# Dense conv of block 1 between the first two tiles of block 0, half of block 0's cast on GpSimd with block 1's memsets behind it, fewer matmuls on zeros

## The chip, the cores and the metric

One core of a Trainium2 chip. The metric is the device time of one execution in microseconds; times quoted are medians over several executions, with lowest and highest. The profile's own span (first to last instruction) is about 1.8 us shorter than the time. Each kernel is compared with executions of the kernel before on the same chip.

## The reference, cut to what matters

```python
# a causal conv over the sequence, 7 taps, one softmaxed kernel for each of 8 heads of 24 channels
out = np.einsum('hk,bskhg->bshg', softmax(weight), x_unfolded)      # x: (8, 4160, 192)
# a maxout feed-forward on each of the 33280 tokens
h = np.maximum(np.maximum(x @ w1, x @ w2), x @ w3)                  # 192 -> 768
return h @ w_out                                                    # 768 -> 192
```

The kernel works in 65 blocks of 512 tokens. For each block it makes the conv as matmuls with a banded matrix, then six tiles of 128 hidden columns ("tiles" below), then the second matrix product. It uses max(a, b, c) = c + max(a-c, b-c, 0): wd holds w1-w3 and w2-w3, one relu on ACT and one max on VectorE (DVE in the profile) finish a tile.

## The kernel before: the parts that matter

The first four blocks are convolved "densely": x is cast from 32 to 16 bits in two interleaved halves xz[t][0] and xz[t][1], each with zeros where the other has data.

```python
def cast_dense(t, copies):                     # copies: an engine for each half
    ...
                    copy(out=xz[t][v]..., in_=xf...)           # 3 operations a half
def conv_dense(t, copies):                     # 60 small matmuls, then three copies to yd on ACT
    ...
def cross(t, cs=range(NC)):                    # VectorE: the other 64 partitions of yd
    ...
def l1(t, j, pools=...):                       # one tile: 6 matmuls, relu on ACT, max on VectorE
    ...
```

The order of the start (every engine works through its own instructions in program order):

```python
    for v in range(2):
        nc.gpsimd.memset(xz[1][v][:], 0.0)     # early, while x is still on its way
    ...
    cast_dense(0, (nc.vector.tensor_copy, nc.scalar.copy))
    ...
    copy_w3(nc.vector.tensor_copy, 0)
    make_wd(0, 1)
    conv_dense(0, (nc.scalar.copy, nc.scalar.copy, nc.scalar.copy))
    keep_warm(4)                               # 4 matmuls on zeros
    cross(0, (0,))
    make_wd(1, 2, nc.gpsimd)
    cross(0, (1, 2))
    l1(0, 0)
    cast_dense(1, (nc.gpsimd.tensor_copy, nc.scalar.copy))
    cast_w3(0)                                 # GpSimd, for the transposes of w3
    copy_w3(nc.vector.tensor_copy, 1)
    l1(0, 1)
    conv_dense(1, (nc.scalar.copy, nc.scalar.copy, nc.scalar.copy))
    keep_warm(3)
    cross(1)
    make_wd(2, 4)                              # VectorE: columns that the third tile needs
    l1(1, 0)
    ...
    l1(0, 2)                                   # "the third tile of block 0" below
```

The softmax here doesn't subtract the row's maximum and nothing guards it: scores larger than these inputs give would overflow.

Of the kernel before, what the change touches and what calls it, by code (L numbers as in the profile page):

```python
# [27 lines left out]
def kernel(  # L28
# [12 lines left out]
    nc = tc.nc  # L41
# [116 lines left out]
    xz = {t: [const.tile([P, NQ, D], FP16, name=f"xz_{t}_{v}") for v in range(2)] for t in range(2)}  # L158
    xz[2], xz[3] = xz[0], xz[1]

    def cast_dense(t, copies):
        xf, _, parts = xin[t]
        for v, copy in enumerate(copies):
            if copy is None:
                continue
            for s in range(CYC // 32):
                cut = GRP * (32 * s // GRP + 1)
                a, b = (32 * s, cut) if v == 0 else (cut, 32 * s + 32)
                for (rl, q0, q1) in parts:
                    copy(  # L170
                        out=xz[t][v][0:rl, q0:q1, :].rearrange("p q (k c) -> p q k c", c=CYC)[:, :, :, a:b],
                        in_=xf[0:rl, q0:q1, :].rearrange("p q (k c) -> p q k c", c=CYC)[:, :, :, a:b])
# [26 lines left out]
    make_identity(nc, ident[:])  # L199
    ident16 = const.tile([P, P], FP16)  # L200
    nc.gpsimd.tensor_copy(out=ident16[:], in_=ident[:])
    for v in range(2):
        nc.gpsimd.memset(xz[1][v][:], 0.0)
    for x16 in x16s + [x16z]:
        w = x16.shape[1] - EDGE
        nc.gpsimd.memset(x16[:, 0:EDGE], 0.0)
# [4 lines left out]
    def keep_warm(n, pool=psw, tag="w"):  # L211

        ps = pool.tile([P, NBLK], FP32, tag=tag, name="idle")
        for _ in range(n):
            nc.tensor.matmul(ps[:], lhsT=idle[:, 0:P], rhs=idle[:], start=True, stop=True)  # L215
# [15 lines left out]
    wrec = const.tile([NHEAD, 1], FP32)  # L231
    nc.vector.reciprocal(out=wrec[:], in_=wsum[:])
    nc.scalar.activation(out=line[:, 31:31 + KW], in_=wexp[:], func=AF.Relu, scale=wrec[:])
    cast_dense(0, (nc.vector.tensor_copy, nc.scalar.copy))
    bps = psq.tile([32, WIN, NHEAD], FP32, tag="q", name="band_cols")
    for c in range(WIN):
        nc.tensor.matmul(bps[:, c, :], lhsT=line[:, WIN - 1 - c:WIN + 31 - c],  # L237
# [14 lines left out]
    def make_wd(j0, j1, eng=nc.vector):  # L252
        f = slice(P * j0, P * j1)
        eng.tensor_sub(out=wd[:, :, f], in0=ws[:, :, f], in1=w3s[:, :, f])  # L254

    def copy_w3(copy, part):
        f = slice(PW * part, PW * (part + 1))
        copy(out=w3s[HALF:P, :, f], in_=w3s[0:HALF, :, f])  # L258

    def cast_w3(part):  # L260
        f = slice(PW * part, PW * (part + 1))
        nc.gpsimd.tensor_copy(out=w3h[:, :, f], in_=w3s[0:HALF, :, f])
# [45 lines left out]
    def conv_dense(t, copies):  # L308


        yd = dense[t] = ydp.tile([P, NC, NBLK], FP16, tag="yd", name=f"yd_{t}")
        for n, slots_ in enumerate((range(4), range(4, 6))):
            ps = psw.tile([P, NBLK], FP32, tag="w", name=f"D{n}_{t}")
            for (q, b, row_lo, rlen, lo, hi, cc) in chunks_of[t]:
                for v in range(2):
                    for g, s in enumerate(slots_):
                        h = (32 * s + 31 * v) // GRP
                        nc.tensor.matmul(  # L318
                            ps[32 * g:32 * g + 32, lo:hi],
                            lhsT=xz[t][v][0:rlen, q, 32 * s:32 * s + 32],  # L320
                            rhs=band[0:rlen, h, cc:cc + hi - lo],
                            start=(v == 0), stop=(v == 1), tile_position=(0, 32 * g))
            if n == 0:
                copies[0](out=yd[0:HALF, 0, :], in_=ps[0:HALF, :])
                copies[1](out=yd[HALF:P, 1, :], in_=ps[HALF:P, :])
            else:
                copies[2](out=yd[0:HALF, 2, :], in_=ps[0:HALF, :])

    def cross(t, cs=range(NC)):

        yd = dense[t]
        for c in cs:
            a, b = (slice(HALF, P), slice(0, HALF))[::-1 if c == 1 else 1]
            nc.vector.tensor_copy(out=yd[a, c, :], in_=yd[b, c, :])  # L334
# [30 lines left out]
    def l1(t, j, pools=((psp, "p"), (psq, "q"))):  # L365


        N, y = blkN[t], dense[t]
        ps = [pool.tile([P, NBLK], FP32, tag=tag, name=f"l{tag}{i}_{t}_{j}")
              for i, (pool, tag) in enumerate(pools)]  # L370
        for c in range(NC):
            for i in range(2):
                row = slice(HALF * i, HALF * (i + 1))
                nc.tensor.matmul(ps[i][:, 0:N], lhsT=wd[row, c, P * j:P * (j + 1)],  # L374
                                 rhs=y[row, c, 0:N],
                                 start=(c == 0), stop=(c == NC - 1))
        r = rp.tile([P, NBLK], FP16, tag="r", name=f"r_{t}_{j}")
        nc.scalar.activation(out=r[:, 0:N], in_=ps[0][:, 0:N], func=AF.Relu)  # L378
        nc.vector.tensor_max(out=hs[t][:, j, 0:N], in0=r[:, 0:N], in1=ps[1][:, 0:N])  # L379
# [81 lines left out]
    copy_w3(nc.vector.tensor_copy, 0)  # L461
    make_wd(0, 1)
    conv_dense(0, (nc.scalar.copy, nc.scalar.copy, nc.scalar.copy))
    keep_warm(4)
    cross(0, (0,))
    make_wd(1, 2, nc.gpsimd)
    cross(0, (1, 2))
    l1(0, 0)
    cast_dense(1, (nc.gpsimd.tensor_copy, nc.scalar.copy))
    cast_w3(0)  # L470
    copy_w3(nc.vector.tensor_copy, 1)
    l1(0, 1)
    conv_dense(1, (nc.scalar.copy, nc.scalar.copy, nc.scalar.copy))
    keep_warm(3)
    cross(1)
    make_wd(2, 4)
    l1(1, 0)
    cast_w3(1)
# [107 lines left out]
```

## Time and profile before

| | before |
|---|---|
| time, median (lowest to highest) | 474.73 us (474.59 to 475.15), 3 runs |
| span of the profiled execution | 472.5 us |
| TensorE's share of the chain that ended last | 98% |
| block 0's first copy to yd on ACT starts | 8.31 us |
| block 1's conv starts | 11.51 us, broken off until 12.17 |
| third tile of block 0 starts | 16.31 us |
| block 2's conv starts | 23.09 us |

The last rows are starts in the timeline of the engine concerned. How much later or earlier block 2's conv starts is the measure used below: behind it TensorE runs from matmul to matmul to the end. The chain, the engines' rows from 9 us on and the arrivals are shown in the prediction. One more piece of the timeline before, VectorE's, from the arrival of block 0's x on (columns: start, duration of the group, engine, line, operation, operands, count, wait before it):

```profile
4.50 0.55 DVE L170 CAST xz<-xf 112x240 f16<-112x240 f32 x3 [1.34 <-DMA xf<-in_x_dram]
5.34 0.69 DVE L258 COPY w3s<-w3s 64x768 f32<-64x768 f32 x1 [0.29 <-DMA w3s<-in_moe_w_dram]
7.42 0.56 DVE L254 TENSOR_TENSOR wd<-ws,w3s 128x384 f16<-128x384 f32 x1 [1.40 <-DMA ws<-in_moe_w_dram]
```

### The profile page before, as it was taken

What the parts mean: (1) busy time and instruction counts of PE and PEld (TensorE: products, weight loads), DVE (VectorE), ACT (ScalarE), POOL (GpSimd) and SP (SyncE); (2) the same over time, 40 slices, a digit from 0 to 9 for tenths busy, and PEclk for the clock granted to TensorE, in tenths of its full rate; (3) what the DMA queues carried; (4) which work ended last, traced back from release to release, by engine and by line L of the source; (5) the groups of instructions that cost most, each with busy time, mean ns of one, the idle gap of its engine ahead of it and who ended that gap; (6) DMA issues with size and microseconds to landing.
All of it is one profiled execution on the core that took longest, in us unless ns stands there. A gap on an engine that the chain in (4) does not pass through costs nothing.

```text
span 472.5 us, 21840 instructions
## 1 busy us (share of the span) xinstructions
PE 467.0 (99%) x9036; PEld 392.1 (83%) x9036; DVE 364.2 (77%) x607; ACT 326.1 (69%) x612; POOL 215.0 (45%) x349
## 2 busy tenths in 40 slices
PE   8999999999999999999999999999999999999996
PEld 4577888888888888888888888888888888888996
DVE  4878878778777787787877877778778787787775
ACT  5777767677676766766667667676676666766664
POOL 5746445345435435354534543543553454454210
PEclk9999999999999999999999999999999999999999
DMA  9956877666577566667666666756675765764423
GB/s 197 242 136 189 211 191 195 171 176 181 166 191 193 162 172 172 163 191 189 166 184 166 194 166 186 192 154 178 173 191 162 199 181 154 195 176 101 108 84 103
DMA packets 68257, 81.49 MB, mean 172 GB/s; under 512 B 9310, under 2 KB 57246, under 8 KB 68158
## 3 DMA queue, kind: packets, MB, share of 16 engines
q1 hardware_dynamic: 55070, 49.21, 42.1%
q0 software_dynamic: 12928, 30.78, 21.3%
q8 instruction: 71, 1.16, 1.1%
q14 instruction: 28, 0.23, 0.2%
q10 hardware_dynamic: 160, 0.10, 0.1%
HBM read 30.31 MB, written 25.56 MB: 118 GB/s over the span
## 4 chain that ended last, share of the span: by engine, by line
PE 98%; DVE 1%; issue 0%; ACT 0%
PE lp L374 32%; PE po L418 30%; PE lq L374 26%; PE G L299 7%; PE idle L215 1%; PE D L318 1%; PE lw L374 1%; DVE yd L334 0%; PE band_cols L237 0%; DVE h L379 0%; DVE w3s L258 0%; PE pm L282 0%; PE pm L278 0%; PE pt L269 0%; DVE o L428 0%
## 5 line engine op out<-in xcount | busy, mean ns | idle before, releaser
L379 DVE TENSOR_TENSOR h<-r,lq 128x512 f16<-128x512 f16 x386 | 264.5, 685 | 97.6 <-ACT r L378 96.6
L378 ACT ACTIVATE r<-lp 128x512 f16<-128x512 f32 x386 | 230.5, 597 | 134.3 <-PE lp L374 89.7
L374 PE MATMUL lp<-yd,wd 64*128 64x512 f16 x1158 | 311.8, 376 | 0.5 <-DVE yd L334 0.5
L374 PE MATMUL lq<-yd,wd 64*128 64x512 f16 x1158 | 311.4, 375 | 0.0
L418 PE MATMUL po<-wo,h 64*128 64x192 f16 x3120 | 230.2, 243 | 0.0
L418 PEld LDWEIGHTS <-h 64*128 64x128 f16 x3120 | 186.2, 94 | 25.8
L374 PEld LDWEIGHTS <-wd 64*128 64x128 f16 x2340 | 164.3, 93 | 21.9 <-issue 1.8
L447 POOL DMA_DIRECT2D out_dram<-o x64 | 51.2, 799 | 235.7 <-DVE o L428 223.7
L357 POOL DMA_DIRECT2D yd<-ys x183 | 92.0, 509 | 1.4 <-ACT ys L344 0.8
L418 PE MATMUL po<-m,yd 64*128 64x192 f16 x780 | 86.9, 243 | 0.0
L428 DVE TENSOR_TENSOR o<-a,po 128x384 f32<-128x384 f32 (+1 forms) x132 | 71.4, 542 | 1.0 <-ACT a L427 1.0
L427 ACT COPY a<-po 128x384 f32<-128x384 f32 (+1 forms) x132 | 61.7, 468 | 2.1 <-PE po L418 2.1
L418 PEld LDWEIGHTS <-yd 64*128 64x128 f16 x780 | 54.8, 94 | 8.1
L151 POOL CAST x<-xf 112x960 f16<-112x960 f32 x60 | 59.6, 995 | 1.5 <-DMA xf<-in_x_dram 1.4
L344 DVE CAST ys<-G 128x512 f16<-128x512 f32 x61 | 39.2, 683 | 0.0
L299 PEld LDWEIGHTS <-x 112*32 112x32 f16 x2400 | 28.6, 96 | 12.7 <-issue 12.3
L344 ACT CAST ys<-G 128x512 f16<-128x512 f32 x61 | 32.9, 588 | 1.3
L299 PE MATMUL G<-band,x 112*32 112x103 f16 (+1 forms) x2400 | 33.3, 209 | 0.0
L215 PE MATMUL idle<-idle 128*128 128x512 f16 x18 | 6.9, 532 | 1.2 <-DVE idle L210 1.2
L318 PEld LDWEIGHTS <-xz 112*32 112x32 f16 x240 | 4.7, 107 | 2.2 <-issue 1.3
L318 PE MATMUL D<-band,xz 112*32 112x103 f16 (+1 forms) x240 | 5.7, 229 | 0.1
L254 POOL TENSOR_TENSOR wd<-ws,w3s 128x384 f16<-128x384 f32 (+1 forms) x2 | 3.2, 1606 | 5.0 <-DMA ws<-in_moe_w_dram 5.0
(52 smaller groups left out, 55.3 us busy)
## 6 DMA issues: line engine op xcount, KB each, us to landing
xf<-in_x_dram SPq DMA_DIRECT2D x57, 420.0 KB, 4.6
out_dram<-o POOLq DMA_DIRECT2D x62, 384.0 KB, 4.2
yd<-yd SPq DMA_DIRECT2D x61, 192.0 KB, 3.1
yd<-ys POOLq DMA_DIRECT2D x61, 48.0 KB, 3.5
yd<-ys SPq DMA_DIRECT2D x61, 48.0 KB, 3.9
xf<-in_x_dram SPq DMA_DIRECT2D x8, 252.0 KB, 4.3
yd<-ys POOLq DMA_DIRECT2D x61, 32.0 KB, 3.3
yd<-ys SPq DMA_DIRECT2D x61, 32.0 KB, 3.6
```

Of the source, the lines that this page charges most:

```text
L151: nc.gpsimd.tensor_copy(out=v[0:rl, q0:q1, :], in_=xf[0:rl, q0:q1, :])
L299: nc.tensor.matmul(G[i][32 * g:32 * g + 32, lo:hi], lhsT=x16[0:rlen, cb:cb + 32], rhs=band[0:rlen, h, cc:cc + hi - lo], start=True, stop=T ...
L318: nc.tensor.matmul(ps[32 * g:32 * g + 32, lo:hi], lhsT=xz[t][v][0:rlen, q, 32 * s:32 * s + 32], rhs=band[0:rlen, h, cc:cc + hi - lo], star ...
L344: copy(out=slots[t][:, i, :], in_=convs[t][i][:])
L357: (nc.sync, nc.gpsimd)[n % 2].dma_start(out=yd[r0:r0 + rows, c, :], in_=slots[t][s0:s0 + rows, half, :])
L374: nc.tensor.matmul(ps[i][:, 0:N], lhsT=wd[row, c, P * j:P * (j + 1)], rhs=y[row, c, 0:N], start=(c == 0), stop=(c == NC - 1))
L378: nc.scalar.activation(out=r[:, 0:N], in_=ps[0][:, 0:N], func=AF.Relu)
L379: nc.vector.tensor_max(out=hs[t][:, j, 0:N], in0=r[:, 0:N], in1=ps[1][:, 0:N])
L418: nc.tensor.matmul(ps[b0, i][:, s % 2, :], lhsT=a, rhs=b, start=first, stop=last)
L427: nc.scalar.copy(out=a[:, ss, :], in_=ps[s0, 0][:, ss, :])
L428: nc.vector.tensor_add(out=outs[t][:, s0:s + 1, :], in0=a[:, ss, :], in1=ps[s0, 1][:, ss, :])
L447: qs[0].dma_start(out=bass.AP(tensor=out.tensor, offset=r * D, ap=[[D, n], [step * D, s1 - s0], [1, D]]), in_=ob[p0:p0 + n, s0:s1, :])
```

## The change

Its intent: ACT is a bottleneck of the start (cast, copies and relus in one queue), so block 0's half cast goes to GpSimd, with the two memsets of block 1's buffers moved from the very start to behind it; block 1's cast and conv move ahead of the second tile of block 0, so that block 1 is ready sooner; and two places get fewer matmuls on zeros.

```diff
-    for v in range(2):
-        nc.gpsimd.memset(xz[1][v][:], 0.0)
...
-    cast_dense(0, (nc.vector.tensor_copy, nc.scalar.copy))
+    cast_dense(0, (nc.vector.tensor_copy, nc.gpsimd.tensor_copy))
+    for v in range(2):
+        nc.gpsimd.memset(xz[1][v][:], 0.0)
...
     conv_dense(0, (nc.scalar.copy, nc.scalar.copy, nc.scalar.copy))
-    keep_warm(4)
+    keep_warm(2)
     cross(0, (0,))
     make_wd(1, 2, nc.gpsimd)
     cross(0, (1, 2))
+    cast_dense(1, (nc.gpsimd.tensor_copy, nc.scalar.copy))
+    copy_w3(nc.vector.tensor_copy, 1)
     l1(0, 0)
-    cast_dense(1, (nc.gpsimd.tensor_copy, nc.scalar.copy))
     cast_w3(0)
-    copy_w3(nc.vector.tensor_copy, 1)
+    conv_dense(1, (nc.scalar.copy, nc.scalar.copy, nc.scalar.copy))
+    cross(1)
     l1(0, 1)
-    conv_dense(1, (nc.scalar.copy, nc.scalar.copy, nc.scalar.copy))
-    keep_warm(3)
-    cross(1)
+    keep_warm(2)
     make_wd(2, 4)
     l1(1, 0)
```

## The prediction

> **What bounds the kernel now.** I read the page first, then the chain of waits in order of time over the first 60 us, then the timelines of ACT, DVE and POOL over the first 24 us. From the page:
>
> ```profile
> PE 467.0 (99%) x9036; PEld 392.1 (83%) x9036; DVE 364.2 (77%) x607; ACT 326.1 (69%) x612; POOL 215.0 (45%) x349
> ...
> PE 98%; DVE 1%; issue 0%; ACT 0%
> ```
>
> TensorE sets the end: 98% of the chain that ended last is matmuls. What isn't TensorE is a per cent or two of 472.5 us, and the diff touches only the start-up, so the question is where in the start-up TensorE stands still. The chain in order of time:
>
> ```profile
> 9.11 0.97 PE idle L215 x4
> ...
> 11.49 0.15 DVE h L379
> 11.65 0.56 issue
> 12.21 0.69 DVE w3s L258
> 12.93 0.69 DVE h L379
> 13.65 0.41 DVE yd L334
> 14.09 0.86 DVE yd L334
> 14.99 0.37 PE lp L374
> ```
>
> Between 11.49 and 14.99 us the chain leaves TensorE; before and after that it stays on it. (9.11 is the first of the two groups of matmuls on zeros that the change shortens; its name is "idle" but TensorE is occupied.) After 14.99 the chain runs from matmul to matmul to the end, with no wait that shows. So a gain is to be had only before about 16 us, and from there on every microsecond gained or lost is carried to the end, unless something else then arrives too late. Why the hole is there, ACT and DVE show:
>
> ```profile
> 10.86 0.60 ACT L378 ACTIVATE r<-lp 128x512 f16<-128x512 f32 x1 [0.76 <-PE lp L374]
> 11.36 0.77 ACT L170 CAST xz<-xf 112x80 f16<-112x80 f32 x3
> ...
> 12.82 0.58 ACT L324 CAST yd<-D 64x512 f16<-64x512 f32 x1 [0.20 <-PE D L318]
> ```
>
> ```profile
> 12.21 0.69 DVE L258 COPY w3s<-w3s 64x768 f32<-64x768 f32 x1
> 12.93 0.69 DVE L379 TENSOR_TENSOR h<-r,lq 128x512 f16<-128x512 f16 x1
> 13.65 1.61 DVE L334 COPY yd<-yd 64x512 f16<-64x512 f16 x3
> 15.29 0.96 DVE L254 TENSOR_TENSOR wd<-ws,w3s 128x768 f16<-128x768 f32 x1
> ```
>
> ACT's half of block 1's cast stands behind the first tile's relu (11.36 to 12.13), so block 1's dense conv begins at 11.51, stops, and goes on only at 12.17. Its three copies to yd end at 14.61, and DVE's three crossings at 15.26. DVE then makes columns 2 to 4 of wd until 16.25; the third tile of block 0 begins at 16.31. TensorE alone would be far ahead of that.
>
> The transfers set a second clock, seen at GpSimd:
>
> ```profile
> 9.72 0.90 POOL L170 CAST xz<-xf 112x240 f16<-112x240 f32 x3 [0.89 <-DMA xf<-in_x_dram]
> 10.57 1.59 POOL L262 CAST w3h<-w3s 64x768 f16<-64x768 f32 x2
> 13.09 0.82 POOL L258 COPY w3s<-w3s 64x768 f32<-64x768 f32 x1 [0.93 <-DMA w3s<-in_moe_w_dram]
> 13.98 0.82 POOL L262 CAST w3h<-w3s 64x768 f16<-64x768 f32 x1
> 16.07 1.84 POOL L254 TENSOR_TENSOR wd<-ws,w3s 128x768 f16<-128x768 f32 x1 [1.28 <-DMA ws<-in_moe_w_dram]
> 18.30 1.14 POOL L491 CAST wo<-wos 128x1152 f16<-128x1152 f32 x1 [0.39 <-DMA wos<-in_moe_w_out_dram]
> 20.01 3.40 POOL L170 CAST xz<-xf 112x240 f16<-112x240 f32 x12 [0.57 <-DMA xf<-in_x_dram]
> ```
>
> These starts are arrivals and won't move. wd's last columns are ready at 17.91 and first used at 19.26 (1.35 us to spare); wo at 19.44, used at 20.71 (1.27); the first six of the twelve casts end near 21.7 and block 2's conv begins at 23.09 (1.4). So TensorE can be at most about 1.27 us earlier whatever the change does.
>
> **What the Trainium skill says.** "SBUF — State Buffer", section "SBUF: two separate sides": VectorE's second pair of SBUF ports is GpSimd's only one, and whoever starts first, a VectorE operation that needs both pairs or a GpSimd one, holds it for the whole instruction. The trace agrees: the crossing copy takes 0.29 us at 8.93 and 9.53, when GpSimd rests, and 0.41 and 0.85 us at 13.65 and 14.09, under GpSimd's copy and cast of w3. "GPSIMD Engine Reference", section "Engine selection": one-input work runs roughly at line rate there. The trace agrees: its three casts of block 1 take 0.90 us, ACT's three of the same shapes 0.78. "TensorE: Matmul & The Clock Gate", "Part 1: The HAM clock gate": matmuls run at half rate until some 3.4 us of activity. The trace: the 512-column matmuls on zeros start 0.43 us apart at 1.2 us, 0.22 apart from 9.04. The change leaves TensorE's order before 9.04 as it was, so I expect the same moment of release, and gaps after it far shorter than 3.4 us.
>
> **The change part by part.**
>
> *Block 0's half cast from ACT to GpSimd, xz[1]'s memset behind it.* ACT loses 0.78 us at 4.45; its band copies then begin at once when the band matmuls end (5.03) instead of at 5.14: 0.1 us. But block 0's conv begins at 7.21, behind five matmuls on zeros that end there, while the band is ready at 6.77. Worth nothing. GpSimd's three casts (0.90) start at 4.45, share the ports with VectorE's three (0.55) and its copy of w3 (0.69), and are over before 6; the two memsets (1.73) end near 7.8. GpSimd's part of wd took 1.37 from 7.46; I read about 0.45 of that as waiting for VectorE's wd (768 columns took 1.84, so 384 should take 0.92), so it ends near 8.8 to 9.2 as before. Its use is after 11.9. Worth nothing either.
>
> *Two matmuls on zeros fewer before the first tile.* They are two of 0.22. But that tile's last matmul waits for the third crossing (10.13 + 0.38 = 10.51). It still starts at 10.56 and ends at 10.77. Worth nothing at the end of the tile.
>
> *Block 1's conv before the second tile.* ACT's casts come right after its third copy of block 0: 10.10 + 0.78 = 10.88 instead of 12.13. GpSimd's casts are done at 10.62. So the conv starts near 10.86, takes 1.03 (block 2's conv, warm: 1.02 in the chain) and ends near 11.9, against 13.1. First copy on ACT at 10.86 + 0.70 = 11.56 (block 2: 23.09 to 23.79), three to 13.35 (0.58 with a pitch of 0.60). That is 1.26 us earlier than 14.61. The second tile follows on TensorE, 11.95 to 12.65 (six matmuls, 0.65 a tile from 17.93, 18.61, 19.26), then two on zeros (0.43).
>
> *DVE, which then sets the pace.* New order: copy of w3's second part, first tile's max, three crossings, second tile's max, wd columns 2 to 4. The copy could begin at 10.53, but its data land near 10.56 (my estimate: between the arrivals at 9.72 and 13.09 lie four equal parts of w3, w1, w2, w3, so a quarter of 3.37 after 9.72) and GpSimd's cast of w3h holds the ports from 10.57 to about 11.25. So: copy to 11.95, max to 12.66, first crossing to 12.97, second to 13.28, third after ACT's 13.35 and behind GpSimd's delayed copy of w3, to 14.15. The second tile's relu on ACT is 13.37 to 13.96; its max 14.17 to 14.86; wd 14.88 to 15.85. The third tile of block 0 starts at 15.9 instead of 16.31. Sum: about -0.4 us. TensorE will have finished block 1's first two tiles and a transpose near 15.2 and wait 0.7 us there: most of the 1.26 us gained on ACT is lost because the second tile's max (0.69) has moved in front of nothing it helped: it now stands between the crossings and wd.
>
> From 15.9 the order of all engines is as before and every deadline above keeps over 0.8 us, so -0.4 us goes through to the end: 474.73 - 0.4 = 474.3.
>
> **The rivals.** (a) No collision on the ports: the copy of w3 runs 10.53 to 11.22, crossings end at 13.70, max runs from 13.98, wd ends at 15.65, the third tile starts at 15.7: -0.6, 474.1. For it: VectorE and GpSimd arrive within 0.05 us of each other, and the first wins. (b) Worse collisions: the copy waits for both casts of w3h (12.16) and two crossings for GpSimd's copy and cast at 13.09 to 14.80. Then the crossings end near 15.2, max 15.9, wd 16.9: +0.6, 475.3. Against it: at 13.65 VectorE got in between two GpSimd instructions (0.41), so one that waits isn't passed over twice. (c) The whole 1.26 us comes through, limited by wo to 1.27: 473.5. That needs wd's columns not to be what the third tile waits for; against it stands wd's end at 16.25 right before the 16.31 start. (d) The gain is hidden by transfers: block 2's conv waits for xz. Against: 1.4 us to spare.
>
> **Range and chances.** From rivals (a) and (b), -0.6 to +0.6 around -0.4, leaning to the gain, with (c) less likely; the three runs before spread 0.56 us. I take 473.5 to 475.0. Two per cent is 9.5 us, eight times what the start-up could give: within 2% at 0.98, 0.01 on either side.
>
> **What would show it right or wrong.** Right: block 0's conv still at 7.2 us; ACT's three casts of block 1 near 10.1; block 1's conv unbroken from about 10.9; ACT's copies of it end near 13.4; the chain goes through DVE (max, wd) just before the third tile of block 0 near 15.9; from there TensorE to the end, all shifted alike. Wrong: block 0's conv late behind GpSimd (its casts held up by VectorE), a crossing longer than 0.8 us, a TensorE wait for wo or for xz between 18 and 24 us, or 512-column matmuls 0.43 us apart after 9.1 us.

## The result, and the profile after

The changed kernel: 474.31 us median (473.60 to 474.67, 4 runs); the kernel before 474.74 (474.59 to 475.15, 4 runs, three of them those of the table above). The ratio of the two is 0.9988 with a 95% interval of 0.9970 to 1.0005. (Ratios are the mean time of one kernel's runs over that of the other's, so not quite the ratio of the medians quoted.) Executions over 1.5% slower than the fastest of the same kernel are left out of the means. The interval includes 1: the 0.43 us between the medians is not secured by these runs alone.

The profiled execution of the changed kernel took 474.56 us, longer than the profiled one of before (474.32). So this trace cannot be expected to show a gain, and it doesn't. Its chain of waits in order of time (start, duration, what):

```profile
1.19 3.48 DMA xf<-in_x_dram
4.80 2.78 DVE xz L170 x2
7.63 1.15 PE D L318 x28
8.80 0.58 ACT yd L324
...
15.04 0.46 DVE h L379
15.64 0.96 DVE wd L254
16.65 0.39 PE lp L374
```

The second half is as predicted: VectorE's max of the second tile, then wd, then the third tile of block 0. The first half is new. Before, the chain ran through matmuls on zeros at this place; now it starts with the arrival of block 0's x (4.80 us), goes through VectorE's cast of it, and block 0's conv can only then go on. VectorE's and GpSimd's rows:

```profile
4.80 2.88 DVE L170 CAST xz<-xf 112x240 f16<-112x240 f32 x3 [1.65 <-DMA xf<-in_x_dram]
7.71 0.69 DVE L258 COPY w3s<-w3s 64x768 f32<-64x768 f32 x1
8.43 0.56 DVE L254 TENSOR_TENSOR wd<-ws,w3s 128x384 f16<-128x384 f32 x1
...
10.83 1.30 DVE L258 COPY w3s<-w3s 64x768 f32<-64x768 f32 x1
12.17 0.69 DVE L379 TENSOR_TENSOR h<-r,lq 128x512 f16<-128x512 f16 x1
12.89 2.12 DVE L334 COPY yd<-yd 64x512 f16<-64x512 f16 x3
15.04 0.69 DVE L379 TENSOR_TENSOR h<-r,lq 128x512 f16<-128x512 f16 x1
15.64 0.95 DVE L254 TENSOR_TENSOR wd<-ws,w3s 128x768 f16<-128x768 f32 x1
```

```profile
4.83 0.98 POOL L170 CAST xz<-xf 112x80 f16<-112x80 f32 x3 [2.80 <-DMA xf<-in_x_dram]
5.75 1.73 POOL L234 MEMSET xz<- 128x960 f16 x2
8.48 1.36 POOL L254 TENSOR_TENSOR wd<-ws,w3s 128x384 f16<-128x384 f32 x1 [1.00 <-DVE w3s L258]
...
10.71 1.84 POOL L262 CAST w3h<-w3s 64x768 f16<-64x768 f32 x2
13.15 0.82 POOL L258 COPY w3s<-w3s 64x768 f32<-64x768 f32 x1 [0.60 <-DMA w3s<-in_moe_w_dram]
14.04 0.82 POOL L262 CAST w3h<-w3s 64x768 f16<-64x768 f32 x1
```

VectorE's three casts take 2.88 us instead of 0.55. Taken one by one, the second of them alone lasts 2.57 (the row gives shortest, median and longest of the three in ns, then first and last start and the shapes):

```profile
L170 DVE CAST xz<-xf x3: 183/285/2572, 4.8 to 7.5; 112x240 f16<-112x240 f32 x1, 112x160 f16<-112x160 f32 x1, 112x80 f16<-112x80 f32 x1
```

It ends at 7.57, just after GpSimd's last memset (7.48). GpSimd's casts and memsets have held it up. Later VectorE's copy of w3 takes 1.30 us (0.69 alone), and three crossings 2.12 (0.87 alone, three times 0.29), each time under GpSimd's casts and copies of w3.

What ACT makes of it:

```profile
8.80 0.58 ACT L324 CAST yd<-D 64x512 f16<-64x512 f32 x1 [2.08 <-PE D L318]
...
10.49 0.78 ACT L170 CAST xz<-xf 112x80 f16<-112x80 f32 x3
11.17 0.59 ACT L378 ACTIVATE r<-lp 128x512 f16<-128x512 f32 x1
11.98 0.58 ACT L324 CAST yd<-D 64x512 f16<-64x512 f32 x1 [0.22 <-PE D L318]
```

Block 0's first copy starts at 8.80 instead of 8.31, block 1's at 11.98 instead of 12.82. So the new order has brought block 1's copies 0.84 us forward even in this execution; of the 1.26 us predicted, the late start of block 0 took about 0.5. Collisions on VectorE then eat more than the 0.84 (the second and third crossing take 0.92 and 0.85 us), and the third tile starts at 16.65 against 16.31. From there on both traces run alike: block 2's conv at 23.44 against 23.09, and the last matmuls of the two end 0.41 us apart.

### The profile page after: what moved, and what is told of

Same layout as the page of the kernel before. It is cut to its first block, busy times and chain, and to the rows that moved or that the text cites. A ratio compares the mean times of both kernels' runs of the same rounds, so it can differ in the third digit from the quotient of the medians.

```text
span 472.8 us, 21832 instructions
## 1 busy us (share of the span) xinstructions
PE 466.7 (99%) x9033; PEld 391.3 (83%) x9033; DVE 367.8 (78%) x607; ACT 325.5 (69%) x609; POOL 217.1 (46%) x352
## 4 chain that ended last, share of the span: by engine, by line
PE 96%; DVE 2%; DMA 1%; issue 1%; ACT 0%; SPq 0%; DVEq 0%
PE lp L374 32%; PE po L418 30%; PE lq L374 26%; PE G L299 7%; DMA xf<-in_x_dram 1%; PE D L318 1%; DVE xz L170 1%; PE lw L374 0%; DVE yd L334 0%; DVE h L379 0%; DVE wd L254 0%; PE pm L282 0%; PE pm L278 0%; ACT yd L327 0%; ACT yd L324 0%
## 5 line engine op out<-in xcount | busy, mean ns | idle before, releaser
L170 POOL CAST xz<-xf 112x80 f16<-112x80 f32 (+2 forms) x18 | 5.2, 334 | 3.3 <-DMA xf<-in_x_dram 2.8
```

## The experiments

Theory P (ports): with GpSimd's cast and memsets beside it, VectorE's cast of block 0 waits until GpSimd rests; block 0's conv then starts a fixed time after x lands. The new order gains what was predicted, the cast's move loses part of it. The rival, theory C (chance): x came late in that one execution (4.80 us instead of 4.45) and the moved cast costs nothing.

All traces in one table, starts in us. "x" is VectorE's first cast of block 0, that is, x's arrival. The text refers to it throughout.

| kernel | x | block 0's first copy | block 1's conv | third tile | block 2's conv |
|---|---|---|---|---|---|
| before | 4.50 | 8.31 | 11.51 | 16.31 | 23.09 |
| before_again | 4.64 | 8.31 | 11.55 | 16.57 | 23.36 |
| changed | 4.80 | 8.80 | 11.27 | 16.65 | 23.44 |
| after_again | 4.62 | 8.64 | 11.10 | 16.51 | 23.30 |
| after_third | 4.67 | 8.69 | 11.36 | 16.56 | 23.35 |
| warm_back | 4.32 | 8.34 | 10.90 | 15.88 | 22.66 |
| order_only | 4.38 | 8.32 | 10.85 | 15.97 | 22.77 |
| order_only_2 | 4.45 | 8.32 | 11.06 | 15.99 | 22.78 |
| memset_early | 4.44 | 7.41 | 10.17 | 15.80 | 22.59 |
| cast_only | 4.25 | 7.87 | 11.20 | 16.59 | 23.38 |
| cast_only_2 | 4.42 | 8.44 | 11.55 | 16.32 | 23.10 |
| w3_pool | 4.33 | 8.32 | 10.83 | 15.87 | 22.66 |
| w3_pool_split | 4.51 | 8.32 | 10.78 | 15.68 | 22.58 |
| memset_twice | 5.14 | 9.13 | 12.47 | 19.25 | 26.04 |

In memset_early and cast_only the five matmuls on zeros ahead of block 0's conv end about 0.5 us earlier than elsewhere (conv from 6.7 instead of 7.2 us), so their second column isn't to be compared with the others'; after_third has that early end too, but there the conv is held up anyway. "The Trainium skill", page "TensorE: Matmul & The Clock Gate", section "Part 1: The HAM clock gate", says that TensorE's full rate comes with a window that runs free of the kernel, so that its moment varies from run to run, by 500 ns either way. These traces agree that it varies, but by more: by their clock records full rate begins at 4.06 to 4.34 us in those three (after_third falls back to half rate from 7.54 to 10.96) and at 8.17 to 12.82 in the other eleven. The five matmuls, 0.22 us apart in the three and 0.43 in the others, say the same.

### The changed kernel again (after_again, after_third)

No edit.

> The changed kernel once more, five rounds, to size the difference. Theory P (ports): with GpSimd casting half of block 0 and then clearing xz[1], VectorE's own cast of block 0 waits until GpSimd rests, and block 0's conv starts when that ends, so its start follows the arrival of block 0's x: 7.2 us when x lands at 4.45, 7.6 when it lands at 4.8. Then its times spread wider than those of before (about 1 us against 0.5), with a median 0.3 to 0.6 us under before. Theory C (chance): the late conv of the first profile was a late arrival and nothing else; then the median is about 1 us under before and a second profile shows VectorE's three casts done in about 0.6 us.

Measured: 474.25 us median of 6, one (481.82) slow; 474.20 for the five fast ones (473.88 to 475.10), against 475.19 of before (11 runs). Ratio 0.9975, interval 0.9955 to 0.9994.

> The changed kernel a third time, for a third trace and more rounds beside order_only. Both traces so far are of runs at the slow end of its times and show block 0's conv held until VectorE's casts end (2.9 us after x lands). Theory P: the same again, whatever the time; median 0.4 to 1 us under before. If the hold is chance, this trace shows casts of 0.6 us.

Measured: 475.80 us median of 6 (474.04 to 478.50) against 475.17; ratio 1.0017, interval 0.9985 to 1.0049. Executions of over 476 us turn up for other kernels on that chip too, before's (476.66, 477.53) and cast_only's; three of these six were such, two of them at a clock of 0.995 and 0.996.

What follows: VectorE's casts took 2.88 us in both traces again, so they are no chance. None of the three profiled executions (474.56, 475.10 and 474.98) is among the kernel's fastest (473.60, 473.88 and 474.04 in the same batches). The median of the fast runs moved from 0.99 under before to 0.63 over it between two batches on one chip: a few executions don't measure half a microsecond here. All eleven fast ones together have a median of 474.81, against 475.17 of before.

### Only the order and the zeros (order_only, order_only_2)

```diff
 # against the changed kernel
+    for v in range(2):
+        nc.gpsimd.memset(xz[1][v][:], 0.0)          # at its old, early place
-    cast_dense(0, (nc.vector.tensor_copy, nc.gpsimd.tensor_copy))
-    for v in range(2):
-        nc.gpsimd.memset(xz[1][v][:], 0.0)
+    cast_dense(0, (nc.vector.tensor_copy, nc.scalar.copy))
```

> Changed kernel with block 0's cast back on ACT and the memsets of xz[1] back at the start: only the new order and the matmuls on zeros are left. Theory P: block 0's conv at 7.2 us unbroken, its first copy on ACT at 8.3 (8.8 in the changed kernel's profile), block 1's conv at 10.9, the third tile of block 0 at 15.9 to 16.2 (16.65), so 0.3 to 0.6 us faster than the changed kernel and 0.6 to 1 faster than before. Theory C: the same time as the changed kernel.

Measured: 474.37 us (473.13 to 475.22, 6 runs) against 475.19; ratio 0.9974, interval 0.9954 to 0.9993.

> Repeat of order_only. Its start was 0.5 to 0.7 us ahead of the changed kernel's in the traces (third tile of block 0 at 15.97 against 16.51 and 16.65), its median was not (474.37 against 474.25). If the lead in the trace reaches the end, this run is 0.3 to 0.6 us faster than after_third; if it is lost later or is chance, within 0.2 us of it.

Measured: 474.40 us (473.69 to 475.93, 6 runs) against 475.17; ratio 0.9979, interval 0.9959 to 0.9999.

In the trace block 0's first copy is at 8.32 again, and the chain of order_only's waits is the predicted one:

```profile
10.92 0.62 PE D L318 x36
11.57 0.58 ACT yd L324
12.18 0.58 ACT yd L325
12.78 0.59 ACT yd L327
...
14.36 0.46 DVE h L379
14.81 0.15 issue
14.96 0.96 DVE wd L254
15.92 0.05 issue
15.97 0.39 PE lp L374
```

Block 1's conv is unbroken from 10.9, ACT's copies follow one another, and max and wd on VectorE release the third tile at 15.97. Block 2's conv starts at 22.77 and 22.78, against 23.09 and 23.36 in the two traces of before and 23.30 to 23.44 in the three of the changed kernel. Of the kernels this is the one with two intervals below 1, though both are held against nearly the same executions of before. It is ahead of the changed kernel by 0.5 to 0.7 us in the traces at block 2's conv. In times, its twelve executions have a median of 474.40 (the changed kernel's eleven fast ones: 474.81); the first batch showed nothing of the lead, the second more than all of it. The direction is what theory P expects; the size in the time is not secured.

### Only the moved cast (cast_only, cast_only_2)

```diff
 # against the kernel before
-    for v in range(2):
-        nc.gpsimd.memset(xz[1][v][:], 0.0)
-    cast_dense(0, (nc.vector.tensor_copy, nc.scalar.copy))
+    cast_dense(0, (nc.vector.tensor_copy, nc.gpsimd.tensor_copy))
+    for v in range(2):
+        nc.gpsimd.memset(xz[1][v][:], 0.0)
```

> Kernel before with only block 0's half cast on GpSimd and the memsets behind it; order and matmuls on zeros as before. Theory P: VectorE's casts of block 0 take over 2 us instead of 0.55, block 0's conv goes on only near 7.5, everything after is that much later: 0.3 to 0.5 us slower than before. Theory C: as before within 0.1 us.

Measured: 476.67 us (476.26 to 477.90, 6 runs) against 475.19; ratio 1.0032, interval 1.0011 to 1.0053. The expectation of 0.3 to 0.5 us slower was missed by a microsecond. Its trace has two waits of TensorE in the steady part, more than any other trace here; the first of them in the chain:

```profile
33.47 4.50 DMA yd<-ys
37.97 0.02 SPq L363
...
38.16 4.90 DMA yd<-yd
```

The two copies that give a block its doubled yd took 4.5 and 4.9 us, and TensorE stood waiting for them (0.4 us here, 0.9 near 350 us).

> Repeat of cast_only, which was 1.5 us slower than before, more than the 0.3 to 0.5 expected; its trace had two stalls of TensorE for late transfers of yd in the steady part (0.4 and 0.9 us), which no other trace has. If those were chance: 0.2 to 0.5 us slower than before. If the cast's move brings them about: again 1.2 us or more slower, with such stalls in the trace.

Measured: 475.26 us (474.94 to 478.83, 6 runs) against 475.17; ratio 1.0013, interval 0.9985 to 1.0040, with one smaller delay of that kind (0.3 us near 40 us). So the 1.5 us of the first batch did not repeat. Why all six executions of that batch were slow stays open; two of them (477.69, 477.90) ran at a clock of 0.995. VectorE's casts took 2.87 and 2.88 us here too, so that part of theory P holds without the new order. In cast_only_2 block 0's first copy is only 0.13 us late (8.44) and block 1's conv not at all (11.55, as in before_again): in the old order there was slack to swallow it.

### The memsets put back, the cast left on GpSimd (memset_early)

```diff
 # against the changed kernel
+    for v in range(2):
+        nc.gpsimd.memset(xz[1][v][:], 0.0)          # at its old, early place
     cast_dense(0, (nc.vector.tensor_copy, nc.gpsimd.tensor_copy))
-    for v in range(2):
-        nc.gpsimd.memset(xz[1][v][:], 0.0)
```

> Changed kernel with the memsets of xz[1] back at the start, the half cast still on GpSimd. If the memsets hold VectorE (theory P with the memsets as its cause): VectorE's casts end at about 6 us, the conv starts unbroken at 7.2, and the time is that of order_only. If GpSimd's three casts alone are enough to hold it: the casts still take over 2 us, and the time is that of the changed kernel.

Measured: 474.51 us (473.99 to 474.64, 5 runs) against 475.19; ratio 0.9977, interval 0.9958 to 0.9995. VectorE and GpSimd in its trace:

```profile
4.44 0.72 DVE L170 CAST xz<-xf 112x240 f16<-112x240 f32 x3 [1.31 <-DMA xf<-in_x_dram]
```

```profile
4.47 0.97 POOL L170 CAST xz<-xf 112x80 f16<-112x80 f32 x3 [0.77 <-DMA xf<-in_x_dram]
```

The same casts on the same two engines at the same time, and VectorE needs 0.72 us; one by one:

```profile
L170 DVE CAST xz<-xf x3: 284/286/313, 4.4 to 4.8; 112x240 f16<-112x240 f32 x1, 112x160 f16<-112x160 f32 x1, 112x80 f16<-112x80 f32 x1
```

So the cast on GpSimd alone need not hold VectorE, while with the memsets behind it VectorE was held in every trace. The time is that of order_only, as expected of that cause. But the memsets' own 1.73 us are not the whole wait: in the changed kernel VectorE's second cast starts at 5.00 and already waits while GpSimd does its second and third cast, before the first memset starts at 5.75. Here, in a single trace, it got in behind GpSimd's first cast (done at 4.93; GpSimd's casts go on to 5.44). Why it is let in here and not there, with starts alike to a few nanoseconds, stays open. What the early memsets do set is how long the wait can last: a VectorE that waited for all three casts, to 5.44, would by my estimate from these durations be done before 6 us, ahead of TensorE at 6.7 or 7.2.

### The matmuls on zeros as before (warm_back)

```diff
 # against the changed kernel
-    keep_warm(2)
+    keep_warm(4)
...
-    keep_warm(2)
+    keep_warm(3)
     make_wd(2, 4)
```

> Changed kernel with four and three matmuls on zeros again instead of two and two. Prediction's step: they lie beside waits for VectorE, so no difference (within 0.2 us). Rival: the two extra ones ahead of the first tile (0.43 us) push it and everything after; then 0.3 us or more slower than after_third. Or they keep TensorE at full rate where two don't: then 512-column matmuls 0.43 us apart show in the changed kernel's trace and not here.

Measured: 474.83 us (474.45 to 475.41, 6 runs) against 475.17; ratio 0.9985, interval 0.9968 to 1.0003. Between the two medians of the changed kernel (474.20 and 475.80), and no later in its trace, so the matmuls on zeros cost nothing that can be seen. Whether they help the rate is less clear. Full rate begins at 9.22 here and at 8.60 in the first trace of the changed kernel, but at 9.95 in after_again and 10.96 in after_third, where the two matmuls on zeros at 9.3 us still start 0.40 us apart. It varies between traces of one kernel too, 9.23 in order_only and 10.65 in order_only_2, and these two reach block 2's conv at 22.77 and 22.78: no cost is seen there.

The trace is worth more for another reason. x landed early (4.32), VectorE's casts took 2.87 us all the same and ended at 7.19, just before TensorE was free at 7.21: nothing was lost, and block 2's conv started at 22.66. Put beside the other traces with the memsets behind the cast, block 0's first copy follows x: 8.34 for x at 4.32, 8.44 for 4.42, 8.64 for 4.62, 8.69 for 4.67, 8.80 for 4.80, always 4.00 to 4.02 us later (leaving out cast_only, where TensorE got to full rate early). Without them it is 8.31 or 8.32 wherever x lands between 4.33 and 4.64 (memset_early aside, for the same reason). This is theory P's fixed time after x.

### The memsets twice (memset_twice)

```diff
 # against the changed kernel
     for v in range(2):
         nc.gpsimd.memset(xz[1][v][:], 0.0)
+        nc.gpsimd.memset(xz[1][v][:], 0.0)
```

> Changed kernel with each memset of xz[1] issued twice: four of 0.86 us behind GpSimd's casts instead of two. In all six traces with the memsets there VectorE's three casts took 2.87 to 2.88 us, and the first copy of block 0 on ACT came 4.02 us after x landed wherever TensorE was not released early. Theory P, VectorE gets the ports only once GpSimd rests: the casts take 2.88 + 1.7 = 4.6 us, the first copy comes 5.7 us after x lands (10.0 to 10.5 instead of 8.3 to 8.8), and since nothing behind it has that much to spare the third tile starts 1.2 to 1.7 later (17.7 to 18.3) and the time is 1.2 to 1.7 us over the changed kernel's. Rival, VectorE is let in after some fixed time or number of operations: the casts still take 2.9 us and the time is that of the changed kernel.

Measured: 475.12 us (474.68 to 478.52, 6 runs) against 475.60; ratio 0.9996, interval 0.9966 to 1.0026. The rival was right and theory P, in the strict form that VectorE waits until GpSimd rests, is refuted. VectorE, then GpSimd:

```profile
5.14 2.85 DVE L170 CAST xz<-xf 112x240 f16<-112x240 f32 x3 [1.99 <-DMA xf<-in_x_dram]
8.02 1.35 DVE L259 COPY w3s<-w3s 64x768 f32<-64x768 f32 x1
...
13.94 3.67 DVE L335 COPY yd<-yd 64x512 f16<-64x512 f16 x3
```

```profile
6.08 0.89 POOL L234 MEMSET xz<- 128x960 f16 x1
7.03 0.90 POOL L235 MEMSET xz<- 128x960 f16 x1
7.87 0.95 POOL L234 MEMSET xz<- 128x960 f16 x1
8.88 1.06 POOL L235 MEMSET xz<- 128x960 f16 x1
```

The casts take 2.85 us, as with two memsets, although GpSimd goes on to 9.94. Taken singly, the second cast is done at 7.07, behind the first memset (its end is 6.97), the third at 7.98, behind the second (7.93), and the copy of w3 at 9.36, during the fourth: VectorE got one operation in at each boundary. With two memsets it wasn't let in between the first and the second in any of six traces (its second cast lasted until both were done). The memsets issued twice on one tile stand 0.06 us apart, the others overlap a little; VectorE's third cast got in at a boundary where they overlap (the second memset ends at 7.93, the third starts at 7.87), so such a pause is not needed. What decides it stays open.

In this trace x landed at 5.14, the latest of all, and one crossing, begun at 14.67, took VectorE 2.6 us under GpSimd's cast and wd; TensorE was at half rate up to 12.82 us as well, and the third tile starts at 19.25. It is an execution of 477.28 us, while four of the six are at 475.12 or below, so this trace's start isn't the usual one.

### A trace of before on another chip (before_again)

No edit.

> The kernel before, run as if it were a change, on the chip of these jobs: a trace of it there and the size of the noise between two equal kernels. Expected: same time within 0.3 us, block 0's first copy at 8.3 us unless TensorE is released early, third tile of block 0 at 16.3, block 2's conv at 23.1. If the third tile starts near 16.0 here too, the lead that order_only's traces show over the first trace of before was the chip's and not the order's.

Measured: 474.86 us (474.41 to 476.94, 6 runs) against 475.20 (11 runs): the same kernel against itself differs by 0.34 us in the median, ratio 0.9996, interval 0.9972 to 1.0021. That is the noise against which all differences here are to be held. Its third tile starts at 16.57, not 16.3: its crossings start 0.12 us later than in the first trace and take 1.75 us instead of 1.61, under GpSimd's work on w3. It ran on chip 9, as the two kernels that follow, while order_only's traces are of chip 10; w3_pool, which differs from order_only in one copy, is at block 2's conv at 22.66 on chip 9. So the kernel before has such losses too, and order_only's lead at block 2's conv is 0.3 to 0.6 us, depending on which of the two traces it is held against.

### Taking work off VectorE's chain (w3_pool, w3_pool_split)

```diff
 # against order_only
-    copy_w3(nc.vector.tensor_copy, 1)
+    copy_w3(nc.gpsimd.tensor_copy, 1)
 # w3_pool_split also
-    make_wd(2, 4)
+    make_wd(2, 3)
+    make_wd(3, 4)
```

> order_only with the copy of w3's second part on GpSimd instead of VectorE. If VectorE's chain (copy, max, crossings, max, wd) is what the third tile waits for: first max near 11.3 instead of 11.8 to 12.0, second max near 13.9, wd done near 15.5, third tile at about 15.6 (15.98 in order_only), 0.3 us faster than order_only. If the chain is set by ACT (copies to 13.4, relu to 13.9): third tile at 15.9, same time.

Measured: 475.04 us (474.14 to 479.20, 6 runs) against 475.20; ratio 1.0003, interval 0.9970 to 1.0037. The first max came at 11.31 as expected, but the third tile only at 15.87, because the crossings then waited for GpSimd, now busy from 9.66 to 14.96 with hardly a pause.

> w3_pool with wd's columns 2 and 3 made by two operations, so that the third tile waits only for the first of them (0.56 us instead of 0.96). Theory as above: third tile at 15.2 to 15.3, where TensorE itself is done; make_m then near 19.6 to 19.7, just behind wo's arrival (19.2 to 19.5): 0.5 to 0.7 us faster than order_only, 1.2 to 1.4 faster than before. If wo comes late (20.35 in one trace), TensorE waits there and the gain beyond 0.4 us is lost.

Measured: 474.42 us (473.77 to 478.01, 6 runs) against 475.20; ratio 0.9989, interval 0.9957 to 1.0022. Third tile at 15.68, not 15.2 to 15.3: the crossings took 2.28 us instead of 0.87. The expected gain over order_only did not come; its 0.78 us under before in the medians is what order_only has (0.77 to 0.82). Among the kernels tried, none is clearly better than order_only, which is below both the kernel before and the changed one in the medians of all its runs, by 0.77 and 0.4 us, though neither by anything near 2%.

## Why the prediction was right or wrong

- **The total.** Predicted 474.3 us, range 473.5 to 475.0; measured 474.31. The figure was right. But its agreement to 0.01 us is luck: the interval of the ratio reaches from 1.4 us faster to 0.2 us slower, and two equal kernels differed by 0.34. The range was also narrower than its reasons: its own rival (b), at 475.3, lies outside it.
- **What bounds the kernel, and that the start alone counts.** Right. From block 2's conv on, all traces run alike (a pair of blocks in 13.95 us on TensorE) but for single waits of 0.2 to 0.9 us for late transfers, and an offset at 23 us is found again at TensorE's last matmul, which ends 445.7 us after block 2's conv starts in nine of the fourteen traces and up to 446.9 in the others. What the prediction did not look at is the rest: from the last matmul to the end of the span it is 3.6 to 4.7 us, a spread of a microsecond. In order_only's first trace the last matmul is 0.26 us earlier than in the first of before (468.49 and 468.75), but the span is 0.2 us longer.
- **"Worth nothing" for block 0's cast on GpSimd.** This step failed. I had the casts "over before 6" and gave the memsets, 1.73 us, a place in time and no effect; with them behind GpSimd's cast, VectorE's second cast waited to the end of all five of GpSimd's operations. VectorE's casts took 2.88 us instead of 0.55, and block 0's conv starts 0 to 0.5 us late depending on when x lands. In the three traces of the changed kernel this took 0.3 to 0.5 us at block 0's first copy, and with the collisions that came after it 0.5 to 0.7 us at block 2's conv against order_only.
- **The rule under it, in rival (b):** "one that waits isn't passed over twice". Wrong: VectorE's second cast was passed over at four ends of GpSimd operations in six of six traces. I had built a rule on one crossing of 0.41 us.
- **Matmuls on zeros, worth nothing.** Nothing in warm_back speaks against it. But I had expected full rate at the same moment in every run. In the trace I had read it begins at 8.97 us, 7.8 us after the first matmul and not the 3.4 quoted, and after_again and after_third still show 0.40 us between matmuls after 9.3, near the 0.43 that I had named as a sign of being wrong. No cost of it is seen at block 2's conv.
- **Block 1's conv before the second tile, -0.4 us.** Right where it is alone: in order_only the conv starts at 10.85 (predicted 10.86), ACT's third copy ends at 13.36 (13.35; 13.71 in its second trace, where the conv starts at 11.06), the third tile starts at 15.97 (15.9), and block 2's conv is 0.3 to 0.6 us earlier than before. That VectorE's second max stands between the crossings and wd and takes most of ACT's gain is seen in the chain, 14.36 to 15.92.
- **How it goes through in the changed kernel.** Only in part as predicted. None of its three traces has the 0.4 us; none of them is of one of its fastest executions. warm_back, the same kernel but for the zeros, has it (block 2's conv at 22.66), with x at 4.32. That the fast executions of the changed kernel (473.6 to 474.3) are those in which x landed early fits all this, but they left no trace: it is argued, not shown. Of the signs of being wrong that I had named, three came: block 0's conv late (with VectorE held by GpSimd, not the other way round), crossings over 0.8 us (0.92 and 0.85 in the first trace), and matmuls near half rate after 9.1 us.
- **Deadlines of the transfers.** Sound as means and too rosy as bounds: wo was ready at 19.44 in the first trace, at 20.35 in order_only, where TensorE began with it at 20.40. The 1.27 us to spare can be gone in a single execution.

So of the two terms of the sum the order came out as predicted or better (0.3 to 0.6 us in the traces, 0.8 in the medians of the times), and the other, put at nothing, was not nothing: the cast with the memsets behind it took 0.5 to 0.7 us back at block 2's conv in the three traces of the changed kernel (nothing in warm_back, where x came early), and the median of the first four executions came out near the 0.4 that had been predicted for the order alone.

## What to carry to other kernels

When work moves to GpSimd, look at what stands behind it in its queue and not only at what moved: here VectorE's casts took some 2.2 us longer with the memsets behind GpSimd's cast than without them (2.88 against 0.72). Clear buffers while the engines still wait for their data. And where the start of a kernel hangs on an arrival that varies by half a microsecond, compare several traces and the same kernel against itself before believing half a microsecond.

## What the Trainium skill lacked or had wrong

- Page "SBUF — State Buffer", sections "SBUF: two separate sides" and "Who interferes with whom": they say that the engine which starts first holds the shared ports for one whole instruction, but not who gets them next when the other is waiting. The runs: with three casts and two memsets back to back on GpSimd, VectorE's second cast waited through all of them (2.57 us, the three casts 2.87 to 2.88 us in six of six traces); with three casts alone (one trace) it got in behind the first, and the three took 0.72 us; with each memset issued twice it got in after the first memset. The wait can be several instructions long, and no page gives a rule for it.
- Page "TensorE: Matmul & The Clock Gate", "Part 1: The HAM clock gate": it names trace events for the two rates and warns that they can be unreliable, but not that a profile can list a granted clock of 1.00 ahead of the first such event: it does so for 0 to 4 us in before, while matmuls on zeros of 512 columns start 0.43 us apart (0.22 from 9.0 us on). Later changes do show: 0.50 for 8 to 9 us in after_third. For the moment of the change from run to run the page gives 500 ns either way; here it lies between 4.06 and 12.82 us.
